# First product of the channel mixing by seven block products in chunks two and three

## The chip, the cores and the metric

The kernel runs on one core of a Trainium2 chip. The metric is the device time of one execution in microseconds (us). The kernel before took 655.24 us, the median of 3 runs (654.52 to 658.01).

Five engines work side by side, each through its own queue in order: PE (matrix products; PEld is its weight load), DVE (vector), ACT (scalar functions, casts, copies), POOL (a second, slower vector engine) and SP (which here only issues DMAs). An engine waits for another by semaphores.

## The reference

Three blocks follow one another on 4 sequences of 576 tokens, 512 channels wide: windowed attention, a gated layer with a spatial product, and a mixer. The change is in the last part of the mixer:

```
def _moe2_ref(x, w_tok1, w_tok2, w_ch1, w_ch2):
    xt = x.transpose(0, 2, 1)
    h = np.maximum(xt @ w_tok1, 0.0) @ w_tok2
    u = x + h.transpose(0, 2, 1)
    h2 = np.maximum(u @ w_ch1, 0.0) @ w_ch2      # w_ch1: 512 x 1536, w_ch2: 1536 x 512
    return (u + h2).astype(np.float32)
```

## The kernel before, in words

Everything is float32. A float32 product is made of three matmuls on rounded words: each operand is split into a high word (ACT rounds it, a CAST) and a low word (DVE subtracts, a TENSOR_TENSOR), and high x high, high x low and low x high are summed in a bank of PSUM (`mm3`, line 155; `split`, lines 141 to 143). The third dimension of a matmul is at most 128, so 512 channels are four steps of three matmuls.

The activations lie in one tile `U`, channels on the partitions, 4 x 2304 tokens. The channel mixing takes the 2304 tokens in three chunks of 768 (`TW`), each in two halves of 384 (`HW`); the chunks are called one, two and three here (c = 0, 1, 2 in the loop of line 760).

In each chunk there are two products. The **first product**, U times W1, is written plainly (`ch1`, lines 722 to 731): W1 has 12 row blocks of 128 (`c1[0..11]`, split once and kept in the tile `ws` for j = 0 to 2 and in tiles `c13`, `c14`, `c15` for j = 3 to 5; block j and block j + 6 lie together), and for each block and each half 12 matmuls of 384 columns go into one of three banks `mm`; ACT takes the bank out with a ReLU (line 729) into a tile `H`. After each j, POOL forms two differences of such tiles (line 734). The **second product**, times W2, already goes by seven block products (`product`, lines 737 to 755): the combinations of W2 were formed beforehand, split, and put in HBM as `scr`; the combinations of the hidden blocks are the differences on POOL. For each of six j a block is split into `oh` (ACT, line 746) and `ol` (DVE, line 747), four buffers each, and six matmuls go into two banks `A` (line 752). The results are added to `U` by DVE or POOL (line 781) and stored.

The weights of the second product come from HBM into the pool `k4`, eight buffers of 128 x 1024 words (line 742). The same pool serves the loading of W1 and W2 before (`load_c1`, `load_c2`, `fetch`), on which DVE works until about 395 us.

The order of instructions up to the end of the attention is written by hand. From there on a scheduler orders each engine's queue when the kernel is built: work that is earlier in the program goes first when its operands and a buffer are there, and later work is put between. In chunks one and two matmuls of the next chunk's first product (line 155) stand between those of the second product (line 752).

Of the kernel before, what the change touches and what calls it, by code (L numbers as in the profile page):

```python
# [20 lines left out]
P = 128  # L21
# [8 lines left out]
def f(ap):  # L30
    return ap.bitcast(F32)
# [3 lines left out]
def tile_kernel(ctx, tc, qT, kT, kE, v, w_in, wsT, b_sp, w_out, w_t1, w_t2, w_c1, w_c2, outT):  # L35
# [20 lines left out]
    bb = const.tile([P, S], F32, name="bb")  # L56
    const.tile([P, 88], F32, name="gap")
# [107 lines left out]
    nat = pool("nat", "right", stack=r_stack, bufs=1)  # L165
    wsp = pool("wsp", "left", bufs=1)
# [475 lines left out]
    scr = tc.dram_tile([8, NJ // 2, P, 2, 2, 256], F32, name="scr")  # L642
    c1 = {}

    def load_c1(j):

        both = ws[:, 2048 * j:2048 * j + 2048] if j < 3 else c1q.tile([P, 2048], F32R, name=f"c1{j}")
        x = k4()
        fetch(x, [w_c1[:, 128 * r:128 * r + 128].rearrange("(k p) c -> p k c", p=P) for r in (j, j + NJ)])
        split(both[:, :1024], both[:, 1024:], x)  # L650
        v = both.rearrange("p (w r k c) -> p w r k c", w=2, r=2, k=4)
        for r in range(2):
            c1[j + NJ * r] = (v[:, 0, r], v[:, 1, r])

# [44 lines left out]
    c1q = pool("c1q", "left", stack=c_stack, bufs=1)  # L699
    up = [pool("up0", "left", stack=c_stack, bufs=1)]  # L700
# [18 lines left out]
    op_ = pool("op", "left", stack=c_stack, bufs=1)  # L719
    Hp = pool("Hp", "right", stack=c_stack, bufs=1)  # L720

    def ch1(u, ft):
# [8 lines left out]
        return out  # L731

# [27 lines left out]
    for c in range(NTOK // TW):  # L760
# [3 lines left out]
        b11, b12, b21, b22, e = [], [], [], [], []  # L764
        for j in range(NJ):
            if c == 0 and j == 0:
                load_c1(5)
                load_c2(5)
            x, y = ch1(u, j)
            b11.append(x)  # L770
            b12.append(y)
            x, y = ch1(u, j + NJ)
            b21.append(x)
            b22.append(y)
            e.append(diff(Hp.tile([P, HW], F32, tag="H", name="H", bufs=30), b12[j], b11[j]))
            diff(b12[j], b22[j], b12[j])
# [121 lines left out]
```

## Time and profile before

| what | value |
| --- | --- |
| median of 3 runs | 655.24 us |
| the profiled execution | 655.88 us, its span 654.0 us |
| mean granted clock of TensorE | 0.990 of full speed |
| busy: PE, DVE, ACT, POOL | 626.1, 407.0, 317.1, 164.0 us |
| first product, chunk one, begins | 366.0 us |
| first product in chunks one to three | 864 matmuls of 128x384 (line 155) |
| second product in chunks one to three | 756 matmuls of 128x384 (lines 752 and 840) |

Busy times are of the whole span. A matmul's own duration in the trace (334 ns) is longer than the distance to the next, since matmuls overlap; what one costs is read from a stretch of them divided by their count. The granted clock is that of PE: 1.00 is the level of 2.4 GHz, 0.50 that of 1.2 GHz.

### The profile page before, as it was taken

What the parts mean: (1) busy time and instruction counts of PE and PEld (TensorE: products, weight loads), DVE (VectorE), ACT (ScalarE), POOL (GpSimd) and SP (SyncE); (2) the same over time, 40 slices, a digit from 0 to 9 for tenths busy, and PEclk for the clock granted to TensorE, in tenths of its full rate; (3) what the DMA queues carried; (4) which work ended last, traced back from release to release, by engine and by line L of the source; (5) the groups of instructions that cost most, each with busy time, mean ns of one, the idle gap of its engine ahead of it and who ended that gap; (6) DMA issues with size and microseconds to landing.
All of it is one profiled execution on the core that took longest, in us unless ns stands there. A gap on an engine that the chain in (4) does not pass through costs nothing.

```text
span 654.0 us, 11885 instructions
## 1 busy us (share of the span) xinstructions
PE 626.1 (96%) x4512; PEld 584.1 (89%) x4512; DVE 407.0 (62%) x861; ACT 317.1 (48%) x809; POOL 164.0 (25%) x172
## 2 busy tenths in 40 slices
PE   6689799999999999999998999999999999999987
PEld 3468699898979898888988999999999999999977
DVE  4786757656485688698899770496300796200892
ACT  4677663535774455566463542454332544232450
POOL 5510000100010010222032164390132570232820
PEclk9889899999999999999998999999999999999999
DMA  8833653322250134534752736177700378500762
GB/s 318 276 96 97 191 165 107 128 74 74 78 174 2 33 115 119 201 113 159 252 184 108 256 114 258 64 217 249 243 0 1 114 215 269 176 1 1 226 215 74
DMA packets 43513, 94.17 MB, mean 144 GB/s; under 512 B 3904, under 2 KB 16448, under 8 KB 43456
## 3 DMA queue, kind: packets, MB, share of 16 engines
q1 hardware_dynamic: 43456, 93.40, 43.1%
q8 instruction: 36, 0.59, 0.4%
q14 instruction: 21, 0.17, 0.1%
HBM read 77.66 MB, written 15.73 MB: 143 GB/s over the span
## 4 chain that ended last, share of the span: by engine, by line
PE 73%; DVE 12%; ACT 7%; DMA 4%; issue 2%; POOL 1%; SPq 0%; DVEq 0%; POOLq 0%; ACTq 0%
PE mm L155 48%; PE A L752 18%; ACT pb L257 3%; DMA k<-in_w_c 3%; PE pt L276 2%; DVE k L68 2%; PE xo L288 1%; DVE k L69 1%; DVE pb L267 1%; DMA U<-in_w_in 1%; POOL k L665 1%; PE sc L234 1%; ACT PT L277 1%; PE A L840 1%; DVE hl L143 1%
## 5 line engine op out<-in xcount | busy, mean ns | idle before, releaser
L747 DVE TENSOR_TENSOR ol<-H,oh 128x384 fp32r<-128x384 f32 x120 | 93.9, 812 | 83.5 <-ACT oh L746 79.0
L734 POOL TENSOR_TENSOR H<-H 128x384 f32<-128x384 f32 x72 | 82.1, 1157 | 147.6 <-ACT H L729 142.2
L752 PE MATMUL A<-oh,w 128*128 128x384 f32 x480 | 108.6, 334 | 0.0
L746 ACT CAST oh<-H 128x384 fp32r<-128x384 f32 x120 | 61.2, 514 | 59.0 <-PE A L752 54.9
L752 PEld LDWEIGHTS A<-oh,w 128*128 128x128 f32 x480 | 85.5, 188 | 0.0
L729 ACT ACTIVATE H<-mm 128x384 f32<-128x384 f32 x72 | 35.1, 491 | 88.6 <-PE mm L155 86.1
L155 PE MATMUL mm<-uh,ws 128*128 128x384 f32 x288 | 76.1, 334 | 0.0
L155 PE MATMUL mm<-uh,c 128*128 128x384 f32 x288 | 73.5, 334 | 0.0
L752 PE MATMUL A<-ol,w 128*128 128x384 f32 x240 | 67.6, 337 | 2.1 <-DVE ol L747 2.1
L155 PE MATMUL mm<-ws,nh 128*128 128x288 f32 x320 | 62.2, 298 | 0.3 <-DVE tmp L385 0.3
L155 PEld LDWEIGHTS mm<-uh,ws 128*128 128x128 f32 x288 | 52.2, 188 | 0.0
L155 PEld LDWEIGHTS mm<-uh,c 128*128 128x128 f32 x288 | 52.0, 188 | 0.0
L155 PEld LDWEIGHTS mm<-ws,nh 128*128 128x128 f32 x320 | 49.9, 188 | 1.1 <-DVE tmp L385 0.6
L354 POOL TENSOR_SCALAR rstd<-mv 128x1 f32<-128x1 f32 x18 | 4.5, 249 | 183.4 <-DVE mv L353 183.2
L155 PE MATMUL mm<-ul,ws 128*128 128x384 f32 x144 | 48.1, 334 | 0.0
L155 PE MATMUL mm<-ul,c 128*128 128x384 f32 x144 | 48.1, 334 | 0.0
L752 PEld LDWEIGHTS A<-ol,w 128*128 128x128 f32 x240 | 43.4, 188 | 3.8 <-DVE ol L747 3.4
L665 POOL TENSOR_TENSOR k<-k 128x256 f32<-128x256 f32 x12 | 13.5, 1136 | 108.3 <-DVE k L69 108.3
L677 DVE TENSOR_TENSOR ul<-U,uh 128x1536 fp32r<-128x1536 f32 x6 | 11.3, 1892 | 43.5 <-PE mm L155 41.7
L155 PE MATMUL mm<-ws,nl 128*128 128x288 f32 x128 | 37.7, 295 | 0.0
L257 ACT ACTIVATE pb<-pb,nm 128x128 f32<-128x128 f32 x96 | 37.2, 398 | 0.4 <-DVE nm L248 0.3
L277 ACT COPY PT<-pt 128x512 f32<-128x512 f32 x36 | 19.5, 591 | 31.2 <-PE pt L276 31.2
(131 smaller groups left out, 1424.7 us busy)
## 6 DMA issues: line engine op xcount, KB each, us to landing
w<-scr SPq DMA_DIRECT2D x63, 512.0 KB, 4.2
k<-in_w_c SPq DMA_DIRECT2D x24, 512.0 KB, 6.4
scr<-hl SPq DMA_DIRECT2D x18, 512.0 KB, 4.1
kk<-in_kT SPq DMA_DIRECT2D x16, 384.0 KB, 4.8
qq<-in_qT SPq DMA_DIRECT2D x18, 256.0 KB, 4.2
va<-in_v SPq DMA_DIRECT2D x18, 256.0 KB, 2.8
vb<-in_v SPq DMA_DIRECT2D x18, 256.0 KB, 3.7
outT<-U SPq DMA_DIRECT2D x24, 192.0 KB, 3.6
```

The lines of the kernel that those rows point to most:

```text
L68: nc.vector.scalar_tensor_tensor(out=y, in0=high, scalar=-0x80000000, in1=y, op0=ALU.bitwise_and, op1=ALU.bitwise_or)
L155: nc.tensor.matmul(o, a, c, start=(i == 0), stop=(i == n - 1))
L257: nc.scalar.activation(out=pb[:, h, :], in_=scs[g][:, h - 4 * g, :] if mk is None else pb[:, h, :], func=AF.Exp, scale=SCALE if mk is None ...
L276: nc.tensor.transpose(pt[:, h, :], pb[:, 4 * g + h, :], ident)
L277: nc.scalar.copy(out=PT[:, 4 * g:4 * g + 4, :], in_=pt)
L665: nc.gpsimd.tensor_tensor(out=blk(o), in0=blk(a), in1=blk(b), op=op)
L677: nc.vector.tensor_tensor(out=ul, in0=us, in1=f(uh), op=ALU.subtract)
L729: nc.scalar.activation(out=t, in_=ps, func=AF.Relu)
L734: nc.gpsimd.tensor_tensor(out=out, in0=a, in1=b, op=ALU.subtract)
L746: nc.scalar.copy(out=oh, in_=blk[j])
L747: nc.vector.tensor_tensor(out=ol, in0=blk[j], in1=f(oh), op=ALU.subtract)
L752: nc.tensor.matmul(acc[d], a, m, start=(first and j == 0 and i == 0), stop=(last and j == NJ - 1 and i == 2), skip_group_check=True)
```

## The change

In chunks two and three the first product too is made by seven block products instead of eight. With W1 seen as 2 x 2 blocks (channels and rows halved: a11, a12, a21, a22 for row blocks j and j + 6) and the chunk's U as 2 x 2 blocks (x11, x21, x12, x22: channels and token halves), four combinations of W1 and four of U are needed. Each block product is two steps of three matmuls (`seven`). Chunk one stays as it was, since the combinations of W1 are made while it runs.

What is added: `sum_c1`, in chunk one, puts W1's blocks together again from their words and forms the four combinations s1 to s4 on DVE, six times, and stores them as float32 in HBM (`sums`). `load_sums` fetches them in chunks two and three and splits them. `usums` forms t1 to t4 of U on DVE and splits them; their words go where they find room: in the half of the second input tile that is no longer split plainly, in the places of a21 in `ws` and `c1b`, and in a small new pool. `ch1_seven` runs the products: banks a and c are from `mm`, b is from `A`; a first product in each bank is read out (ACT copies it as p1, DVE adds p1 and keeps x and z) before a second is summed on top. To make room, `bb` moves to another pool, the tiles of W1 for j = 3 to 5 become one tile, and a gap shrinks. The lines of the changed kernel are shifted: `seven` is 782, the additions of DVE 807 to 826, the second product 848 and 853.

```diff
-        both = ws[:, 2048 * j:2048 * j + 2048] if j < 3 else c1q.tile([P, 2048], F32R, name=f"c1{j}")
+        both = c1_words(j)
...
+    def sum_c1(j):
+        hl = f(c1_words(j))
+        x, y = [k4() for _ in range(2)]
+        nc.vector.tensor_tensor(out=x, in0=hl[:, :1024], in1=hl[:, 1024:], op=ALU.add)
+        a11, a12, a21, a22 = [x[:, 256 * i:256 * i + 256] for i in range(4)]
+        s1, s2, s3, s4 = [y[:, 256 * i:256 * i + 256] for i in range(4)]
+        for o, a, b, op in ((s1, a21, a22, ALU.add), (s3, a11, a21, ALU.subtract), (s2, s1, a11, ALU.subtract), (s4, a12, s2, ALU.subtract)):
+            nc.vector.tensor_tensor(out=o, in0=a, in1=b, op=op)
+        nc.sync.dma_start(out=sums[j], in_=y.rearrange("p (s c) -> p s c", s=4))
+
+    def load_sums(j):
+        x = k4()
+        nc.sync.dma_start(out=x.rearrange("p (s c) -> p s c", s=4), in_=sums[j])
+        h, l = [kp.tile([P, 1024], F32R, tag="k4", name=n, bufs=8) for n in ("sh", "sl")]
+        split(h, l, x)
...
-        nc.scalar.copy(out=uh, in_=us)
-        nc.vector.tensor_tensor(out=ul, in0=us, in1=f(uh), op=ALU.subtract)
+        k0 = 2 if c and h else 0
+        split(uh[:, k0:], ul[:, k0:], us[:, k0:])
         return uh, ul
+
+    def usums(c, u):
...
+        t1, t2, t3, t4 = [k4()[:, :2 * HW].rearrange("p (k c) -> p k c", k=2) for _ in range(4)]
+        for i, o, a, b in ((0, t1, x12, x11), (1, t2, x22, t1), (2, t3, x22, x12), (3, t4, x21, t2)):
+            nc.vector.tensor_tensor(out=o, in0=a, in1=b, op=ALU.subtract)
+            split(*homes[i], thirds(o))
...
+    def seven(o, ws2, us2, first):
+        todo = [x for (sh, sl), (mh, ml) in zip(ws2, us2) for x in ((sh, mh), (sh, ml), (sl, mh))]
+        for i, (a, m) in enumerate(todo):
+            nc.tensor.matmul(o, a, m, start=first and i == 0, stop=i == len(todo) - 1, skip_group_check=True)
...
+    def ch1_seven(X):
+        x11, x21, x22, t1, t2, t3, t4 = X
+        S = [load_sums(j) for j in range(2)]
+        outs, left = [], []
+        for j in range(NJ):
+            if j and j + 1 < NJ:
+                S.append(load_sums(j + 1))
+            s1, s2, s3, s4 = S[j]
+            a, c = [psmm.tile([P, 512], F32, tag="mm", name="mm")[:, :HW] for _ in range(2)]
+            b = psA.tile([P, 512], F32, tag="A", name="A")[:, :HW]
...
+            seven(a, a11, x11, True)
+            p1 = op_.tile([P, HW], F32, tag="p1", name="p1", bufs=2)
+            nc.scalar.copy(out=p1, in_=a)
+            seven(b, s2, t2, True)
+            for step in left:
+                step()
+            x, z = [op_.tile([P, HW], F32, tag=t, name=n, bufs=4) for t, n in (("oh", "x"), ("ol", "z"))]
+            nc.vector.tensor_tensor(out=x, in0=b, in1=p1, op=ALU.add)
+            seven(c, s1, t1, True)
+            nc.vector.tensor_tensor(out=z, in0=c, in1=p1, op=ALU.add)
+            seven(a, a12, x21, False)
+            nc.scalar.activation(out=h11, in_=a, func=AF.Relu)
+            seven(b, s3, t3, False)
+            def total(o, bank, more):
+                nc.vector.tensor_tensor(out=o, in0=bank, in1=more, op=ALU.add)
+                nc.scalar.activation(out=o, in_=o, func=AF.Relu)
+            total(h22, b, z)
+            seven(c, s4, x22, False)
+            total(h12, c, x)
+            e = diff(H(), h12, h11)
+            diff(h12, h22, h12)
+            def last(b=b, a22=a22, h21=h21, p1=p1):
+                seven(b, a22, t4, False)
+                nc.vector.tensor_tensor(out=h21, in0=b, in1=p1, op=ALU.add)
+                nc.scalar.activation(out=h21, in_=h21, func=AF.Relu)
+            left = [last]
...
+        if c:
+            b11, b12, b21, b22, e = ch1_seven(usums(c, u))
+        else:
...
+                if j:
+                    sum_c1(j - 1)
+            sum_c1(NJ - 1)
```

Up to the middle of chunk one the queue of every engine keeps its order. From there on they differ, at three places as follows.

DVE's queue of the kernel before, at the end of chunk one's first product (`hl` are W2's words for HBM, `ol` low words for the second product, `ul` those of chunk two's input):

```order
L143 TENSOR_TENSOR hl<-k_4528,hl 128x256
L143 TENSOR_TENSOR hl<-k_4528,hl 128x2x256
L747 TENSOR_TENSOR ol<-H,oh 128x384
L143 TENSOR_TENSOR hl<-k_4529,hl 128x2x256 x2
L747 TENSOR_TENSOR ol<-H,oh 128x384
L677 TENSOR_TENSOR ul<-U,uh 128x1536 x2
L747 TENSOR_TENSOR ol<-H,oh 128x384 x11
```

The same place in the changed kernel, where the combinations of W1 (lines 663 and 667, the last of six shown) have been put in:

```order
L667 TENSOR_TENSOR k_4903<-k_4903,k_4902 128x256
L667 TENSOR_TENSOR k_4974<-k_4973 128x256 x2
L663 TENSOR_TENSOR k_4981<-c1b 128x1024
L667 TENSOR_TENSOR k_4903<-k_4902,k_4903 128x256
L667 TENSOR_TENSOR k_4974<-k_4974,k_4973 128x256
L667 TENSOR_TENSOR k_4982<-k_4981 128x256 x2
L667 TENSOR_TENSOR k_4974<-k_4973,k_4974 128x256
L667 TENSOR_TENSOR k_4982<-k_4982,k_4981 128x256
L667 TENSOR_TENSOR k_4982<-k_4981,k_4982 128x256
L142 TENSOR_TENSOR ul<-U,uh 128x1536
L142 TENSOR_TENSOR ul<-U,uh 128x768
L848 TENSOR_TENSOR ol<-H,oh 128x384 x11
```

Six groups of five additions now stand ahead of the two splits of the next input and of the fifth low word of the second product; the second of these splits is half as wide.

DVE's queue of the kernel before, in the sixth block product of chunk one (low words, here with their numbers, and additions to `U`):

```order
L747 TENSOR_TENSOR ol_5312<-H_4604,oh_5311 128x384
L747 TENSOR_TENSOR ol_5322<-H_4667,oh_5321 128x384
L747 TENSOR_TENSOR ol_5334<-H_4730,oh_5333 128x384
L781 TENSOR_TENSOR U_84<-A_5237,U_84 128x384
L781 TENSOR_TENSOR U_84<-A_5238,U_84 128x384
L747 TENSOR_TENSOR ol_5344<-H_4793,oh_5343 128x384
L747 TENSOR_TENSOR ol_5356<-H_4856,oh_5355 128x384
L747 TENSOR_TENSOR ol_5366<-H_4919,oh_5365 128x384
L747 TENSOR_TENSOR ol_5382<-H_4619,oh_5381 128x384
```

The same place in the changed kernel (line 720 forms T; `ul_5504` is the low word of t1):

```order
L848 TENSOR_TENSOR ol_5362<-H_4606,oh_5361 128x384
L720 TENSOR_TENSOR k4_5509<-U_83 128x768
L848 TENSOR_TENSOR ol_5372<-H_4669,oh_5371 128x384
L848 TENSOR_TENSOR ol_5384<-H_4740,oh_5383 128x384
L888 TENSOR_TENSOR U_83<-A_5287,U_83 128x384
L142 TENSOR_TENSOR ul_5504<-k4_5509,uh_5503 128x768
L888 TENSOR_TENSOR U_83<-A_5288,U_83 128x384
L720 TENSOR_TENSOR k4_5510<-U_83,k4_5509 128x768
L848 TENSOR_TENSOR ol_5394<-H_4811,oh_5393 128x384
L848 TENSOR_TENSOR ol_5406<-H_4882,oh_5405 128x384
L720 TENSOR_TENSOR k4_5511<-U_83 128x768
L848 TENSOR_TENSOR ol_5416<-H_4953,oh_5415 128x384
```

T's eight instructions stand between the low words of the last two block products, one by one; the first four are seen here.

PE's queue of the kernel before, in the last block product of chunk one (`mm` is the next chunk's first product):

```order
L752 MATMUL A_5237<-oh_5403,w_5401 128x384 x2
L752 MATMUL A_5238<-oh_5403,w_5401 128x384 x2
L752 MATMUL A_5237<-ol_5404,w_5401 128x384
L752 MATMUL A_5238<-ol_5404,w_5401 128x384
L752 MATMUL A_5237<-oh_5413,w_5401 128x384 x2
L752 MATMUL A_5238<-oh_5413,w_5401 128x384 x2
L155 MATMUL mm_5502<-ul_5454,ws_98 128x384
L155 MATMUL mm_5502<-uh_5453,ws_98 128x384
L752 MATMUL A_5237<-ol_5414,w_5401 128x384
L752 MATMUL A_5238<-ol_5414,w_5401 128x384
L752 MATMUL A_5237<-oh_5425,w_5423 128x384 x2
L752 MATMUL A_5237<-ol_5426,w_5423 128x384
```

The changed kernel, from the third row block of that product on:

```order
L853 MATMUL A_5287<-oh_5453,w_5451 128x384 x2
L853 MATMUL A_5288<-oh_5453,w_5451 128x384 x2
L782 MATMUL A_5539<-ws_98,sh_5527 128x384 x2
L782 MATMUL mm_5538<-uh_5503,sh_5527 128x384
L782 MATMUL mm_5538<-ul_5504,sh_5527 128x384
L782 MATMUL mm_5600<-uh_5499,ws_98 128x384
L782 MATMUL mm_5600<-ul_5500,ws_98 128x384
L782 MATMUL mm_5600<-uh_5499,ws_98 128x384 x2
L782 MATMUL mm_5600<-ul_5500,ws_98 128x384
L782 MATMUL mm_5600<-uh_5499,ws_98 128x384
L853 MATMUL A_5287<-ol_5454,w_5451 128x384
L853 MATMUL A_5288<-ol_5454,w_5451 128x384
```

The matmuls put between are now ten at once, four on the first sums (`sh`) and six on the first input block of the second row block.

## Rows read from the trace of the kernel before

**Rows 1.** Page, busy time of each engine (share of the span) and instructions:
```profile
PE 626.1 (96%) x4512; PEld 584.1 (89%) x4512; DVE 407.0 (62%) x861; ACT 317.1 (48%) x809; POOL 164.0 (25%) x172
```

**Rows 2.** Windows: start:end, length, busy (count) per engine, clock, DMA:
```profile
408.00:414.00 6.00, 6.00 (x36) 6.00 (x35) 0.00 (x0) 1.27 (x3) 2.03 (x2) 1.00 0.00 0
...
426.00:432.00 6.00, 6.00 (x36) 6.00 (x35) 6.00 (x6) 2.59 (x6) 6.00 (x6) 1.00 0.77 238
...
450.00:456.00 6.00, 6.00 (x36) 6.00 (x36) 3.63 (x7) 3.20 (x7) 0.00 (x0) 1.00 0.69 207
...
480.00:486.00 6.00, 6.00 (x36) 6.00 (x35) 0.25 (x1) 1.48 (x3) 1.52 (x2) 1.00 0.00 0
...
618.00:624.00 6.00, 5.27 (x29) 4.51 (x27) 6.00 (x5) 2.27 (x5) 6.00 (x6) 1.00 0.69 236
...
624.00:630.00 6.00, 4.62 (x23) 3.99 (x24) 6.00 (x12) 4.44 (x10) 1.31 (x2) 1.00 0.41 153
```

**Rows 3.** Chain that ended last: start us, us, engine, tile, line, instructions:
```profile
354.80 61.28 PE mm L155 x360
...
561.90 41.60 PE mm L155 x240
...
620.50 1.37 DVE ol L143
```

**Rows 4.** Waits of PE, 355 to 654 us: total us, times, longest:
```profile
PE A L752 <- DVE ol L747: 2.1, 4, 0.7
```

**Rows 5.** Tiles ol and U: count: duration ns min/median/max, first and last start:
```profile
L747 DVE TENSOR_TENSOR ol<-H,oh x120: 541/559/1416, 370.0 to 640.4; 128x384 fp32r<-128x384 f32 x120
L781 DVE TENSOR_TENSOR U<-A,U x36: 540/548/558, 433.1 to 650.5; 128x384 f32<-128x384 f32 x36
```

**Rows 6.** Groups by form: count, busy us, mean ns, idle before and releaser:
```profile
L143 DVE TENSOR_TENSOR ws<-k,ws 128x1024 fp32r<-128x1024 f32 x3 | 3.7, 1217 | 0.0
...
L143 DVE TENSOR_TENSOR c<-k,c 128x1024 fp32r<-128x1024 f32 x3 | 4.5, 1491 | 0.3 <-ACT c L142 0.3
...
L143 DVE TENSOR_TENSOR t_l<-k,t_h 128x512 fp32r<-128x512 f32 x2 | 1.4, 682 | 0.0
...
L143 DVE TENSOR_TENSOR t_l<-k,t_h 128x256 fp32r<-128x256 f32 x1 | 0.4, 419 | 0.0
...
L143 DVE TENSOR_TENSOR hl<-k,hl 128x256 fp32r<-128x256 f32 x6 | 4.2, 707 | 0.0
...
L142 ACT CAST ws<-k 128x1024 fp32r<-128x1024 f32 x3 | 3.2, 1054 | 3.5 <-DVE k L69 3.5
...
L729 ACT ACTIVATE H<-mm 128x384 f32<-128x384 f32 x72 | 35.1, 491 | 88.6 <-PE mm L155 86.1 <-POOL H L734 2.4
...
L791 ACT COPY p<-A 128x384 f32<-128x384 f32 x6 | 2.8, 477 | 1.0 <-PE A L752 1.0
```

**Rows 7.** Timeline of DVE: start us, us, instruction, count, idle before it:
```profile
390.93 2.11 DVE L143 TENSOR_TENSOR hl<-k,hl 128x512 fp32r<-128x512 f32 x2 [3.91 <-ACT hl L142]
...
394.30 1.00 DVE L747 TENSOR_TENSOR ol<-H,oh 128x384 fp32r<-128x384 f32 x1 [1.26 <-ACT oh L746]
...
415.92 1.76 DVE L677 TENSOR_TENSOR ul<-U,uh 128x1536 fp32r<-128x1536 f32 x1 [20.62 <-PE mm L155]
...
425.37 7.84 DVE L747 TENSOR_TENSOR ol<-H,oh 128x384 fp32r<-128x384 f32 x6 [0.48 <-PE A L752]
```

**Rows 8.** Window of line L155 (first product) alone, 420 to 444 us:
```profile
420.00:444.00 24.00, 6.97 (x30) 5.26 (x30) 1.00 0.63 200
```

**Rows 9.** Windows around the idle time of PE before 356 us:
```profile
352.00:354.00 2.00, 0.83 (x7) 0.78 (x6) 2.00 (x5) 0.15 (x1) 0.10 (x1) 1.00 0.00 0
354.00:356.00 2.00, 1.49 (x8) 1.25 (x7) 2.00 (x6) 0.88 (x2) 1.92 (x3) 0.70 0.00 0
356.00:358.00 2.00, 2.00 (x10) 2.00 (x10) 1.43 (x2) 0.94 (x2) 1.57 (x2) 0.50 0.34 132
```

**Rows 10.** DMA issues: tensors, queue, count, KB each, median us to landing:
```profile
w<-scr SPq DMA_DIRECT2D x63, 512.0 KB, 4.2
```

More of the change, by code (lines that the diff above doesn't have):

```diff
@@ L55, in tile_kernel @@
     nc.gpsimd.memset(mhalf, -0.5)
-    bb = const.tile([P, S], F32, name="bb")
-    const.tile([P, 88], F32, name="gap")
+    const.tile([P, 24], F32, name="gap")
     U = const.tile([P, 4, NTOK], F32, name="U")
@@ L642, in tile_kernel, with c1_words @@
     scr = tc.dram_tile([8, NJ // 2, P, 2, 2, 256], F32, name="scr")
+    sums = tc.dram_tile([NJ, P, 4, 256], F32, name="sums")
     c1 = {}
+    def c1_words(j):
+        return (ws if j < 3 else c1b)[:, 2048 * (j % 3):2048 * (j % 3) + 2048]
     def load_c1(j):
-        both = ws[:, 2048 * j:2048 * j + 2048] if j < 3 else c1q.tile([P, 2048], F32R, name=f"c1{j}")
+        both = c1_words(j)
         x = k4()
@@ L653, in load_c1 @@
             c1[j + NJ * r] = (v[:, 0, r], v[:, 1, r])
+    def sum_c1(j):
[12 more added lines that the diff above has]
+        split(h, l, x)
+        return [[(h[:, 256 * i + 128 * k:256 * i + 128 * k + 128], l[:, 256 * i + 128 * k:256 * i + 128 * k + 128]) for k in range(2)] for i in range(4)]
     def load_c2(j):
@@ L719, in tile_kernel @@
     op_ = pool("op", "left", stack=c_stack, bufs=1)
+    tq = pool("tq", "left", stack=c_stack, bufs=1)
     Hp = pool("Hp", "right", stack=c_stack, bufs=1)
@@ L731, in ch1, with H @@
         return out
+    def seven(o, ws2, us2, first):
+        todo = [x for (sh, sl), (mh, ml) in zip(ws2, us2) for x in ((sh, mh), (sh, ml), (sl, mh))]
+        for i, (a, m) in enumerate(todo):
+            nc.tensor.matmul(o, a, m, start=first and i == 0, stop=i == len(todo) - 1, skip_group_check=True)
+    def H():
+        return Hp.tile([P, HW], F32, tag="H", name="H", bufs=30)
+    def ch1_seven(X):
[8 more added lines that the diff above has]
+            b = psA.tile([P, 512], F32, tag="A", name="A")[:, :HW]
+            a11, a12, a22 = [[(c1[r][0][:, k, :], c1[r][1][:, k, :]) for k in ks] for r, ks in ((j, (0, 1)), (j, (2, 3)), (j + NJ, (2, 3)))]
+            h11, h12, h21, h22 = [H() for _ in range(4)]
+            seven(a, a11, x11, True)
[24 more added lines that the diff above has]
+            left = [last]
+            outs.append((h11, h12, h21, h22, e))
+        left[0]()
+        return [list(x) for x in zip(*outs)]
@@ L763, in tile_kernel @@
         u += [uin(c, h) for h in range(len(u), 2)]
[L764 to L776, printed above, removed]
+        if c:
+            b11, b12, b21, b22, e = ch1_seven(usums(c, u))
+        else:
+            b11, b12, b21, b22, e = [], [], [], [], []
+            for j in range(NJ):
+                if j == 0:
+                    load_c1(5)
+                    load_c2(5)
+                x, y = ch1(u, j)
+                b11.append(x)
+                b12.append(y)
+                x, y = ch1(u, j + NJ)
+                b21.append(x)
+                b22.append(y)
+                e.append(diff(H(), b12[j], b11[j]))
+                diff(b12[j], b22[j], b12[j])
+                if j:
+                    sum_c1(j - 1)
+            sum_c1(NJ - 1)
         us = [[U[:, 2 * dh:2 * dh + 2, t0 + HW * h:t0 + HW * h + HW] for h in range(2)] for dh in range(2)]
```

13 lines of the change are left out of this document (added).

## The prediction

> **What bounds the kernel now.** I read the page first, then the span cut into windows, then the chain that ended last, then the waits of TensorE. The page gives PE 96% of the span [rows 1]. In the windows the reader is to see that from about 366 us on PE is busy for the whole of nearly every stretch at a granted clock of 1.00, while DVE goes from nothing (408 to 414) to all of its time (426 to 432) and back to almost nothing (480 to 486) [rows 2]. The chain says the same: it is PE alone from 354.80 us on, broken only in the last chunk, and 240 matmuls of the first channel product take 41.60 us, so one costs 0.1733 us whenever nothing delays it [rows 3]. The waits of PE after 355 us hold one entry of weight: 2.1 us in 4 waits of the second product for DVE's low words, all four in the last chunk, the only one without the matmuls of a next chunk to put in between [rows 2, 4]. So this part of the kernel is a queue of matmuls: 540 for a chunk (288 in the first product, 252 in the second), and a matmul less is worth 0.1733 us as long as the other engines keep PE fed.
>
> **The change part by part.** Dropping multiplications: the first product of a chunk before is 12 row blocks times 2 halves times 12 matmuls, 288. Now it is 6 times 7 block products of 6 matmuls, 252, of the same 384 columns. Over two chunks that is 72 matmuls less: 72 x 0.1733 = 12.48 us [rows 3]. No matmul is added anywhere, and chunk one keeps its 288. This is the whole of the gain, and everything below is what may be paid back.
>
> The combinations of W1 (chunk one): DVE gets six times a 1024-wide addition and four 256-wide ones. With 1.217 us for 1024 columns and 0.419 for 256 that is 6 x (1.217 + 4 x 0.419) = 17.4 us; with the dearest rows of these widths (1.491 and 0.707) it is 25.9 us [rows 6]. In the order they stand ahead of the splits of chunk two's input and of the fifth low word of the second product. DVE stood idle there from the end of its split at 395.3 us to 415.92 us, 20.6 us, and could begin some 2 us earlier [rows 7]. At the lower price they are over by about 411 us and cost nothing; at the upper one they end some 3 to 5 us after 416. Behind the last of them wait the input's splits, then the fifth low word. PE has four blocks of the second product ready, 4 x 6 x 0.1733 = 4.2 us, and the 6 matmuls of chunk two that need only the first input block; the second input split is half as wide as before, which gives back 0.9 us. So about 2 us of delay is covered, and what can show is 0 to 4 us. I take 0.5, near the lower price, because POOL is mostly idle there: from 408 to 414 it has 2.03 of 6 us [rows 2]. The six stores of the sums go to SP's queue ahead of the weights of the second product; those land 4.2 us after issue [rows 10] and have 20 us.
>
> Less to put in between: while POOL works without a pause, a low-word split takes 1.3 us (six in 7.84 us from 425.37) in place of its median 0.559 [rows 5, 7], which is more than the 1.04 us PE needs for the block. Before, PE filled the time with matmuls of the next chunk, 30 between 420 and 444 us [rows 8]. Now there are 12, since the other six products need operands that are formed later. The nearest row for a chunk without any such filling is the last chunk, which lost 2.1 us [rows 4], with two of the final block's extra splits in the same stretch. Bounds per chunk are 0 and 2.1 us; below nothing is excluded, since PE is full there already. With 12 matmuls (2.1 us) left, and without the extra splits, I am near nothing: 0.5 for each of chunks one and two, 1.0 in all.
>
> Forming T (at the end of chunks one and two): per chunk DVE gets four subtractions and four splits 768 wide, less half of one input split, and the first two splits of W1's sums. A 768-wide one lies between 0.682 (512) and 1.217 (1024) [rows 6], 0.95 in the middle: 8 x 0.95 + 2 x 1.217 = 10.0 us, next to 12 low-word splits (6.7 us) and four additions to the residual (2.2 us) during the last two products of the chunk. That is 18.9 us of DVE against 12.5 us of second-product matmuls and 28 matmuls of chunk two that the order puts there, 4.9 us: 17.4. POOL has nothing in that stretch (0.00 from 450 to 456) [rows 2], and PE enters it with up to four blocks in hand, which is 4.2 us. So the deficit of 1.5 us is covered on paper; an early subtraction in front of a low word can still show. Bounds per chunk 0 and 3.7 us (if 768 columns cost as much as 1024 beside a busy POOL, 8 x (1.491 - 0.95) = 4.3 more, and only half the lead is there, 2.1); I take 0.75, so 1.5 in all.
>
> The seven products themselves (chunks two and three): a bank now goes PE, DVE, PE up to three times. Per row block DVE gets five additions with one operand in PSUM and a 1024-wide split: 5 x 0.55 + 1.217 = 4.0 us, and ScalarE a copy, four ReLUs and a 1024-wide cast: 0.477 + 4 x 0.491 + 1.054 = 3.5 us [rows 5, 6], against 42 x 0.1733 = 7.3 us of PE. Both fit. The additions out of PSUM are the right kind: that form takes 540 to 558 ns in all 36 runs, POOL busy or not, while the split of two SBUF operands goes from 541 to 1416 [rows 5]. The order leaves 12 or more matmuls, 2.1 us, between a product into a bank and the next one into it, where the addition and its place in DVE's queue (a 1.2 us split ahead of it at worst) take 1.8 us. Bounds: nothing, and the longest single wait of the last chunk, 0.7 us [rows 4], in each of 12 row blocks, 8.4. I take 0.75 a chunk, 1.5 in all, nearer to the row of the additions.
>
> The loads of the sums, six a chunk, stand in SP's queue behind the stores of finished outputs and ahead of the next chunk's weights, whose prefetch was done during the first product with all eight buffers free. Now the buffers come free as sums are used up. The first weights are wanted some 40 us after the stage begins and the last sums are split well before, so 4.2 us of landing [rows 10] are hidden; if not, one landing a chunk, 8.4 us, shows.
>
> Sum: 12.48 - 0.5 - 1.0 - 1.5 - 1.5 = 8.0 us. The profiled execution took 655.88 us (span 654.0), so it would take 647.9; the median of the runs shown is 0.64 lower, 655.24, and the forecast 647.2.
>
> **The rivals.** First, everything is covered: PE stays full in chunks two and three, and 12.5 us are kept, with at most 2.5 lost: 642.8 to 645.2. For it speaks that PE lost nothing in chunks one and two before, with DVE at 6.00 of 6 us; against it that the margins above are a few matmuls wide, where they were dozens.
>
> Second, the gain is eaten: each of the 12 row blocks shows one wait of 0.7 us, and the T's and the landing of weights add their upper bounds in part: 8.4 + 3 to 5 us paid, 655.24 - 12.5 + 11.4 to 13.4 = 654.1 to 656.1. For it speaks the strict order on DVE, where an addition PE needs stands behind casts it does not need yet; against it the half-empty DVE (4.0 of 7.3 us).
>
> Third, the other side: the clock. Where PE idled 1.68 us between 352 and 356 us, its granted clock read 0.70 and then 0.50 in the 4 us from 354 on [rows 9], the lower level of 1.2 GHz: 0.6 + 1.0 = 1.6 us more, so that such a gap costs 3.3 us. If the round trips of the seven products open one gap of that size in every second row block, six in all, 20 us are paid: 655.24 - 12.5 + 20 = 662.7, slower; it decides from five such gaps on. Against it: the four waits of the last chunk, 0.7 us at the longest, left the clock at 1.00 [rows 2, 4], and the order has other products at hand. The Trainium skill (TensorE: Matmul & The Clock Gate, "A second HAM failure mode: psum-queue depth-cycling") holds that cycling through PSUM banks with small idles between groups of matmuls makes the clock swing between its levels; taken at its word it speaks for this rival even with gaps of 0.7 us, and the last chunk's trace, with the clock at 1.00, does not agree for four of them.
>
> That the change does not do what it says can be left out for the multiplications: the order of the changed program has 252 matmuls there.
>
> **How the numbers follow.** What a measurement of this kernel can tell from no change is about 0.5%, 3.3 us: faster means under 651.9, slower over 658.5. The forecast (645.2 to 651.9) has 0.55, the first rival 0.22, the second with its neighbourhood (651.9 to 658.5) 0.14, the third 0.09. So faster 0.77, same 0.14, slower 0.09. The range runs from 643.3, where of all costs only some 0.5 us shows, to 653.0, a little into the second rival; some 0.04 lie below it and 0.16 above.
>
> **What would show it.** Right: 252 matmuls of the first product in some 44 us in chunks two and three, where 288 took 50; PE waits for DVE of 2 to 6 us beside the old 2.1; the clock at 1.00; DVE busy from 393 to about 412 us without PE noticing; the 128x384 additions out of PSUM at 0.55 us. Wrong: PE waits on the new additions of 0.5 us and more in each row block, a granted clock under 1.00 after 420 us, low-word splits of the last two products late behind the T's by more than 2 us, or PE waiting for weights or sums to land.

## The result and the profile after

The changed kernel takes **648.73 us**, the median of 4 runs (648.16 to 650.56), against 655.25 us for the kernel before (654.52 to 658.01): a ratio of 0.9898, 95% interval 0.9863 to 0.9933. The profiled execution took 650.56 us, its span 648.4 us, at a mean granted clock of 0.989.

**The whole.** The page of the changed kernel, busy time of each engine, share of the span and instructions:

```profile
PE 617.8 (95%) x4440; PEld 571.0 (88%) x4440; DVE 489.7 (76%) x979; ACT 337.2 (52%) x841; POOL 171.1 (26%) x172
```

TensorE has 72 matmuls less than in [rows 1], and DVE 82.7 us more work. What this bought is best measured over one stretch, from the end of chunk one's first product to the end of the span, since ahead of it PE does the same work in both programs. The chain that ended last, of the changed kernel (start, duration, engine, tile, line, instructions):

```profile
356.87 61.28 PE mm L154 x360
```

Chunk one's first product ends at 356.87 + 61.28 = 418.15 us; before it ended at 354.80 + 61.28 = 416.08 us [rows 3]. The stretch behind it was 654.0 - 416.1 = 237.9 us and is 648.4 - 418.15 = 230.25 us: **7.7 us shorter** (forecast 8.0). The piece of 360 matmuls that the first product ends takes the same 61.28 us; it begins 2.1 us later, for a reason that lies ahead of it. Windows around that start, of the changed kernel (start:end, length, busy and count of PE, PEld, DVE, ACT and POOL, granted clock, DMA share, GB/s):

```profile
352.00:354.00 2.00, 0.67 (x6) 0.44 (x4) 2.00 (x4) 0.32 (x1) 0.00 (x0) 1.00 0.00 0
354.00:356.00 2.00, 0.70 (x5) 0.70 (x6) 2.00 (x5) 0.08 (x1) 0.02 (x1) 1.00 0.00 0
356.00:358.00 2.00, 1.49 (x9) 1.26 (x8) 2.00 (x6) 0.95 (x2) 1.92 (x3) 0.85 0.00 0
358.00:360.00 2.00, 2.00 (x11) 2.00 (x10) 1.78 (x4) 0.85 (x2) 1.66 (x2) 0.50 0.34 131
```

PE is idle for 3.14 of the 6 us up to 358, and then the clock is granted at 0.85 and 0.50; in [rows 9] the same gap held 1.68 us. The queues of both programs are the same there, and the chain names the late data: a load of W1 that was issued 0.35 us later and took 1.73 us longer to land, which makes the 2.1 us. Its piece of the chain, before and after:

```profile
337.53 5.26 DMA k<-in_w_c
337.88 6.99 DMA k<-in_w_c
```

So this is one execution's late data and not the change. A second profiled execution of the changed kernel (first run below) ended the same product at 411.59 us, and its stretch behind it was 641.7 - 411.59 = 230.1 us. It had a gap too: PE was busy for 0.55 and 1.49 us of the two windows of 2 us from 348, so 1.96 us idle, but there the granted clock stayed at 1.00. The end of that product moves by 6.6 us between two executions of one program; the stretch agrees to 0.2.

**The stretch, in order.** Windows of the changed kernel, columns as above:

```profile
414.00:420.00 6.00, 6.00 (x36) 6.00 (x36) 4.84 (x9) 3.98 (x6) 3.17 (x2) 1.00 0.92 267
420.00:426.00 6.00, 6.00 (x37) 6.00 (x36) 5.44 (x6) 2.89 (x7) 3.19 (x3) 1.00 1.02 417
...
438.00:444.00 6.00, 5.92 (x32) 5.14 (x31) 6.00 (x8) 2.85 (x6) 3.37 (x3) 1.00 0.68 238
...
450.00:456.00 6.00, 6.00 (x37) 6.00 (x35) 5.86 (x10) 4.05 (x8) 0.00 (x0) 1.00 0.33 126
456.00:462.00 6.00, 6.00 (x36) 6.00 (x36) 6.00 (x11) 5.09 (x9) 0.00 (x0) 1.00 0.36 115
...
480.00:486.00 6.00, 6.00 (x36) 5.88 (x36) 3.59 (x8) 3.58 (x7) 2.03 (x2) 1.00 0.00 0
...
516.00:522.00 6.00, 6.00 (x29) 4.57 (x28) 6.00 (x6) 3.18 (x7) 6.00 (x5) 1.00 0.76 246
522.00:528.00 6.00, 5.30 (x30) 4.64 (x29) 6.00 (x7) 2.11 (x5) 6.00 (x6) 1.00 0.52 173
...
612.00:618.00 6.00, 5.08 (x25) 3.94 (x25) 6.00 (x7) 0.93 (x2) 6.00 (x5) 1.00 0.62 210
618.00:624.00 6.00, 4.45 (x24) 3.81 (x23) 6.00 (x12) 5.12 (x12) 1.35 (x2) 1.00 0.37 122
```

The reader is to look at the counts behind PE, not at its busy time: a full window of 6 us holds 36 or 37 matmuls. From 516 to 522 us PE is "busy" for all of it and still issues 29. Where W1's combinations (414 to 420), T (450 to 462) and the seven products (480 to 486) were feared, the windows are full; where the second product's low words are made beside a working POOL, they are not. Summed over neighbouring windows, chunk one lacks 5 matmuls (0.9 us), chunk two some 17 (3.0 us) and chunk three some 26 (4.6 us). Before, only chunk three lacked any: 29 and 23 in the two windows of [rows 2] against 36.5 full, 21 in all or 3.6 us. The granted clock is 1.00 in all of these. DVE is busy for the whole of the windows with the fewest matmuls (438, 516, 522, 612, 618), so it does not stand there waiting for differences that POOL delivers late.

The waits of PE in the changed kernel, 355 to 654 us (total us, times, longest):

```profile
PE A L853 <- DVE ol L848: 3.2, 5, 1.2
PE mm L154 <- DVE U L639: 3.1, 2, 2.6
```

The first line answers to [rows 4]: the same wait, 1.1 us longer. It shows 3.2 us where the counts show 8.5 lost. The second line is the gap before the first product. What was lost stands in another list, the waits of the weight load (PEld); from 410 us to the end, of the changed kernel and of the kernel before:

```profile
PEld A L853 <- DVE ol L848: 8.9, 20, 1.5
PEld A L752 <- DVE ol L747: 3.4, 4, 1.0
```

It is PE's weight load that waits for the low words, 8.9 us in 20 waits where the counts say 8.5, and 3.4 before where they say 3.6.

The groups by form in the changed kernel (count, busy us, mean ns, idle before and releaser):

```profile
L848 DVE TENSOR_TENSOR ol<-H,oh 128x384 fp32r<-128x384 f32 x120 | 98.9, 863 | 7.4 <-ACT oh L847 6.6 <-ACT p L898 0.6
L835 POOL TENSOR_TENSOR H<-H 128x384 f32<-128x384 f32 x72 | 89.3, 1257 | 136.2 <-ACT H L816 103.1 <-ACT H L775 28.2 <-DVE ol L848 4.0
...
L888 DVE TENSOR_TENSOR U<-A,U 128x384 f32<-128x384 f32 x36 | 18.6, 550 | 8.3 <-PE A L947 4.1 <-PE A L853 3.9
...
L720 DVE TENSOR_TENSOR k<-U 128x768 f32<-128x768 f32 x4 | 3.8, 953 | 0.5 <-PE A L853 0.5
```

Low words (median 558 ns, as in [rows 5]) have a mean of 863: a part of them takes twice as long or more (1407 ns at most). Additions to `U` with an operand in PSUM stay at 550, and T's subtractions at 953, as estimated. POOL's stretch and what DVE does beside it, in chunk two (start, us, instruction, count, idle before), first POOL:

```profile
501.24 7.40 POOL L835 TENSOR_TENSOR H<-H 128x384 f32<-128x384 f32 x5 [3.98 <-ACT H L816]
509.13 6.83 POOL L835 TENSOR_TENSOR H<-H 128x384 f32<-128x384 f32 x5 [0.49 <-DVE ol L848]
515.93 7.75 POOL L888 TENSOR_TENSOR U<-p,U 128x384 f32<-128x384 f32 x6
523.64 7.46 POOL L835 TENSOR_TENSOR H<-H 128x384 f32<-128x384 f32 x6
```

then DVE:

```profile
512.89 11.21 DVE L848 TENSOR_TENSOR ol<-H,oh 128x384 fp32r<-128x384 f32 x9
524.02 1.01 DVE L888 TENSOR_TENSOR U<-A,U 128x384 f32<-128x384 f32 x2
524.95 7.03 DVE L848 TENSOR_TENSOR ol<-H,oh 128x384 fp32r<-128x384 f32 x6
```

POOL runs 30 us with a single pause of 0.49. Nine low words take 11.21 us, 1.25 each, and six of POOL's additions 7.75, 1.29 each: beside each other, each engine finishes one every 1.25 to 1.3 us. PE needs 1.04 us for the six matmuls of one low word, so DVE can't keep up, and the additions to `U` between them, 0.55 us, are not touched. In the kernel before, most of POOL's differences of this chunk came one or two at a time while the plain first product ran, and the unbroken stretch behind them was 16 us:

```profile
510.45 1.81 POOL L734 TENSOR_TENSOR H<-H 128x384 f32<-128x384 f32 x1 [3.21 <-ACT H L729]
514.43 2.55 POOL L734 TENSOR_TENSOR H<-H 128x384 f32<-128x384 f32 x2 [2.16 <-DVE ol L747]
519.04 7.46 POOL L781 TENSOR_TENSOR U<-p,U 128x384 f32<-128x384 f32 x6 [2.06 <-ACT p L791]
526.47 8.74 POOL L734 TENSOR_TENSOR H<-H 128x384 f32<-128x384 f32 x7
```

Of the chunk's 24 differences 16 lie in the unbroken stretch of the changed kernel, from 501.24 on, and 10 lay behind 510.45 before: POOL carries more of them on into the second product. That the seven products finish the hidden blocks later is read from the program; it was not tried.

### The profile page after: what moved, and what is told of

Its sections match the earlier page's. It is cut to its first block, busy times and chain, and to the rows that moved or that the text cites. A ratio compares the mean times of both kernels' runs of the same rounds, so it can differ in the third digit from the quotient of the medians.

```text
span 648.4 us, 11947 instructions
## 1 busy us (share of the span) xinstructions
PE 617.8 (95%) x4440; PEld 571.0 (88%) x4440; DVE 489.7 (76%) x979; ACT 337.2 (52%) x841; POOL 171.1 (26%) x172
## 4 chain that ended last, share of the span: by engine, by line
PE 62%; DVE 17%; DMA 7%; ACT 7%; issue 4%; POOL 1%; SPq 1%; DVEq 0%; POOLq 0%; ACTq 0%
PE mm L154 27%; PE A L853 16%; PE mm L782 8%; PE A L782 6%; DMA k<-in_w_c 4%; ACT pb L257 4%; DVE ol L848 2%; DVE k L67 2%; DVE k L68 2%; PE pt L276 2%; PE xo L288 2%; DVE gl L598 1%; DVE pb L267 1%; POOL k L688 1%; DMA raw<-in_wsT 1%
## 5 line engine op out<-in xcount | busy, mean ns | idle before, releaser
L835 POOL TENSOR_TENSOR H<-H 128x384 f32<-128x384 f32 x72 | 89.3, 1257 | 136.2 <-ACT H L816 103.1
L848 DVE TENSOR_TENSOR ol<-H,oh 128x384 fp32r<-128x384 f32 x120 | 98.9, 863 | 7.4 <-ACT oh L847 6.6
L265 DVE TENSOR_SCALAR rs<-sm 128x8 f32<-128x8 f32 (+1 forms) x19 | 3.7, 196 | 47.5 <-ACT pb L257 47.5
L71 ACT ACTIVATE k<-k 128x512 f32<-128x512 f32 (+2 forms) x31 | 19.7, 645 | 28.5 <-DMA k<-in_w_c 22.9
L154 PE MATMUL mm<-xh,wi_h 128*128 128x384 f32 x96 | 32.7, 341 | 0.7 <-ACT vf L348 0.6
L154 PE MATMUL mm<-xh,wi_l 128*128 128x384 f32 x96 | 32.1, 335 | 0.0
L154 PE MATMUL mm<-xl,wi_h 128*128 128x384 f32 x96 | 32.1, 334 | 0.0
L154 PE MATMUL mm<-gh,wo_h 128*128 128x512 f32 (+1 forms) x80 | 29.7, 375 | 0.0
L154 PE MATMUL mm<-gl,wo_h 128*128 128x512 f32 (+1 forms) x80 | 29.6, 370 | 0.0
L154 PE MATMUL mm<-gh,wo_l 128*128 128x512 f32 (+1 forms) x80 | 29.5, 369 | 0.0
```

The lines of the kernel that those rows point to most:

```text
L71: nc.scalar.activation(out=x, in_=f(high), func=AF.Copy, scale=DOWN)
L154: nc.tensor.matmul(o, a, c, start=(i == 0), stop=(i == n - 1))
L835: nc.gpsimd.tensor_tensor(out=out, in0=a, in1=b, op=ALU.subtract)
L848: nc.vector.tensor_tensor(out=ol, in0=blk[j], in1=f(oh), op=ALU.subtract)
```

## The experiments

Theory: the 72 matmuls are saved in full, and what is paid back comes from one place, DVE's low words beside POOL. Rivals: the new places of the tiles, the round trips of the banks, or T have a price of their own. Stretches are measured as above, from the end of chunk one's first product in each run's profile.

**The changed kernel again**, unaltered, beside the next experiments.

> The changed kernel once more, unaltered, as the base on this chip for the runs beside it. Theory and rivals alike: 648 to 649 us if this chip is like the first, 0.988 to 0.992 of the kernel before.

650.22 us (643.83 to 652.48, 10 runs), ratio 0.9916 [0.9882, 0.995] to the kernel before on that chip (654.74); the time is 1.2 us above the expected 649, the ratio inside the expected range. The profiled execution, 643.83, is the shortest of the ten and the one told of above: with a stretch of 230.1 us, what it is ahead by lies before the stretch. Differences of 2 us between medians of different chips are not read below; stretches are.

**The places alone.** The first product is plain in all chunks; tiles, pools and lines are those of the changed kernel.

```diff
-        k0 = 2 if c and h else 0
+        k0 = 0
...
-        if c:
+        if False:
             b11, b12, b21, b22, e = ch1_seven(usums(c, u))
...
-                if j:
-                    sum_c1(j - 1)
-            sum_c1(NJ - 1)
```

> The changed kernel with the plain first product in all three chunks, so that of the change only the new places of tiles are left (the bias row in another pool, the smaller gap, W1's last three blocks in one tile). Theory (the new places cost nothing, and the 2 us by which the profiled execution after began the first product later is one late load of W1): as the kernel before, 655.2 us, at most 1 us off, and the first product beginning within 1 us of 366.0. Rival (the new places delay the stage before the mixing): 657.3 us, every run some 2 us above the kernel before.

654.62 us (650.78 to 656.93, 10 runs), ratio 1.0 [0.9973, 1.0026]. Stretch 653.3 - 415.28 = 238.0 us, before 237.9. The new places cost nothing, the rival's 657.3 is out, and the later start of the first product does not come from them.

**The six additions of POOL left out** in each chunk (the first block product's share of the output is then missing in three of its quarters).

```diff
-        for d in range(2):
-            p1 = op_.tile([P, HW], F32, tag="p1", name="p1", bufs=2)
-            nc.scalar.copy(out=p1, in_=A[d])
-            for dh, h in ((0, 1), (1, 1), (1, 0)):
-                accum(dh, h, d, p1, nc.gpsimd)
```

> The changed kernel without the six additions to U on POOL in each chunk (left out: the first block product is not added to three of the four quarters of the output), with their two copies on ScalarE. Theory (what is lost of the 12.5 us is lost where POOL and DVE work on SBUF together in the second product, 0.9, 3.0 and 4.6 us in chunks one to three): 7.5 us of POOL a chunk are gone, the low words there go back to 0.55 us, PE's waits fall under 2 us in all, and the time is 642 to 644 us. Rival (the loss comes from the new work on DVE, the T's and the round trips of the seven products): these are untouched, 647.5 to 649 us.

639.44 us (638.59 to 646.78, 5 runs), ratio 0.9783 [0.9758, 0.9807]: a larger gain than the theory's 642 to 644, and the rival's 647.5 to 649 is out. In chunk two every window is full again; in chunk three one still lacks 7 matmuls. The profiled execution, 646.78, is the longest of the five, and shows a price that neither profile of the changed kernel has. Its wait of PE and two windows:

```profile
PE A L853 <- DMA w<-scr: 2.7, 1, 2.7
```

```profile
414.00:420.00 6.00, 5.14 (x30) 4.82 (x28) 5.85 (x8) 4.00 (x6) 2.52 (x2) 1.00 0.84 249
420.00:426.00 6.00, 4.15 (x17) 4.15 (x18) 2.40 (x5) 1.02 (x2) 2.21 (x2) 0.77 1.02 416
```

The stores of W1's sums and the weights of the second product go out together, and the DMA engines are full; the weights came late, PE stood for 2.7 us, and the clock was granted at 0.77 in the window with the wait's end: some 26 matmuls fewer than two full windows hold, 4.5 us. The execution is 6 to 8 us longer than the other four, which were not profiled, so the rest of that is open. Its stretch is 644.9 - 417.05 = 227.9 us with these 4.5 in it.

**The same six additions by DVE, straight from PSUM.**

```diff
-            p1 = op_.tile([P, HW], F32, tag="p1", name="p1", bufs=2)
-            nc.scalar.copy(out=p1, in_=A[d])
             for dh, h in ((0, 1), (1, 1), (1, 0)):
-                accum(dh, h, d, p1, nc.gpsimd)
+                accum(dh, h, d, A[d])
```

> The changed kernel with those six additions on DVE, straight from the PSUM bank, so that nothing is left out. Theory (contention with POOL): DVE gets 6 x 0.55 = 3.3 us more a chunk but six low words get 0.75 us shorter, 4.5 us, and POOL is free 7.5 us earlier for the differences: 644.5 to 647 us. Rival (DVE's amount of work in that stretch is what counts, with or without POOL): 3.3 us more in each chunk where DVE is full, 651 to 655 us.

645.61 us (645.06 to 646.55, 4 runs), ratio 0.9878 [0.9859, 0.9897]: inside the theory's 644.5 to 647, and the rival's 651 to 655 is out. Stretch 643.5 - 416.4 = 227.1 us, 3.1 less than the changed kernel's. Chunk one is full but for a wait of 0.2 us for weights at its start; one window of chunk two (28 matmuls) and three of chunk three (32, 29, 29) are not. DVE has six additions, 3.3 us, more to do in each chunk, and PE still loses less.

**x and z added twice**: six times two more additions out of PSUM in each of chunks two and three, 6.6 us of DVE, inside the round trip of the banks.

```diff
-            nc.vector.tensor_tensor(out=x, in0=b, in1=p1, op=ALU.add)
+            for _ in range(2):
+                nc.vector.tensor_tensor(out=x, in0=b, in1=p1, op=ALU.add)
             seven(c, s1, t1, True)
-            nc.vector.tensor_tensor(out=z, in0=c, in1=p1, op=ALU.add)
+            for _ in range(2):
+                nc.vector.tensor_tensor(out=z, in0=c, in1=p1, op=ALU.add)
```

> The changed kernel with the two additions that stand between two products into one bank (x and z) each done twice, 1.1 us of DVE more in each of the 12 row blocks, on the way from PE to DVE and back to PE. Theory (the seven products have slack, DVE is busy some 26 of 42 us there): no change beyond 1 us, 647.5 to 649.5. Rival (the round trips are tight and part of what is lost): 0.55 to 1.1 us a row block, 655 to 662 us.

650.64 us (649.62 to 654.65, 10 runs), ratio 0.9951 [0.9927, 0.9974]: 2.3 to 3.5 us more than the changed kernel's two ratios give, with intervals that overlap. The profiled stretch is clearer: 647.8 - 412.2 = 235.6 us, 5.4 more than the changed kernel's. The theory's "no change beyond 1 us" fell, and the rival's 655 to 662 did not come either. Its waits of PE from 415 us on:

```profile
PE A L855 <- DVE ol L850: 3.6, 7, 0.8
PE A L782 <- ACT sh L141: 2.5, 2, 1.5
PE A L855 <- DMA w<-scr: 1.9, 1, 1.9
```

None of them is on x or z (lines 807 to 811), and the windows inside the seven products are full (36 or 37 matmuls): the round trips held with twice the additions. What shows is the first sums (`sh`) at the hand-over from the second product to the seven, once in each of chunks two and three, where the counts lack some 18 matmuls, 3.1 us; and once the late weights again, some 12 matmuls or 2.2 us. The doubling did not test the hand-over alone, so why the first sums are late in this order is not shown.

**T formed twice**: the four subtractions of line 720, 0.95 us each, are repeated, 3.8 us of DVE in each of two chunks.

```diff
-            nc.vector.tensor_tensor(out=o, in0=a, in1=b, op=ALU.subtract)
+            for _ in range(2):
+                nc.vector.tensor_tensor(out=o, in0=a, in1=b, op=ALU.subtract)
             split(*homes[i], thirds(o))
```

> The changed kernel with each of the four subtractions that form the T's done twice: 4 x 0.95 = 3.8 us of DVE more at the end of chunks one and two, where POOL is idle and PE stayed full. Theory (forming the T's is covered, some 3.7 us of DVE are idle between 444 and 474 us): 0 to 1.5 us a chunk, 648 to 651 us. Rival (the T's stand on the path already and their doubling shows in full): 3.8 us a chunk, 656 us.

655.25 us (652.48 to 657.48, 10 runs), ratio 1.0012 [0.9986, 1.0037], 5.0 us above the changed kernel on that chip: my expectation of 648 to 651 fell. The time is near the rival's 656, but the doubling does not show in full, as the rival has it: stretch 651.3 - 415.2 = 236.1 us, 5.8 more, of 2 x 3.8 = 7.6 put in. Windows of this kernel where T is formed in chunk one:

```profile
450.00:456.00 6.00, 5.88 (x34) 5.57 (x33) 6.00 (x11) 2.97 (x7) 0.00 (x0) 1.00 0.18 66
456.00:462.00 6.00, 5.01 (x29) 4.69 (x28) 6.00 (x11) 3.25 (x6) 0.00 (x0) 1.00 0.45 153
462.00:468.00 6.00, 5.72 (x34) 5.23 (x32) 4.63 (x7) 2.16 (x3) 0.00 (x0) 1.00 0.53 145
```

The changed kernel had 37, 36 and 37 there. T costs nothing as it is, and by this estimate has about (7.6 - 5.8) / 2 = 0.9 us to spare in a chunk.

**Half of POOL's differences on DVE too** (on top of the additions: lines with b11, b22 and b21, b11).

```diff
         for j in range(NJ):
-            diff(b11[j], b22[j], e[j])
+            ddiff(b11[j], b22[j], e[j])
...
-            diff(b21[j], b21[j], b11[j])
+            ddiff(b21[j], b21[j], b11[j])
```

> The kernel with the POOL additions on DVE, and besides the twelve differences of b11 and b21 in each chunk on DVE. Theory (a POOL instruction costs DVE about 0.75 us by holding up a split, a difference on DVE itself costs 0.55): another 2.4 us a chunk of DVE gained, PE's waits under 2 us, 642 to 645 us. Rival (DVE's own amount decides, 6.6 us more a chunk in the full stretch): 649 to 656 us.

643.67 us (642.64 to 644.27, 4 runs), ratio 0.9834 [0.9794, 0.9874]: inside the theory's 642 to 645, and the rival's 649 to 656 is out. Stretch 642.0 - 417.55 = 224.45 us. Low words have a mean of 589 ns.

**All of them on DVE, POOL without work in the mixing.**

```diff
     def diff(out, a, b):
-        nc.gpsimd.tensor_tensor(out=out, in0=a, in1=b, op=ALU.subtract)
+        nc.vector.tensor_tensor(out=out, in0=a, in1=b, op=ALU.subtract)
...
-                accum(dh, h, d, p1, nc.gpsimd)
+                accum(dh, h, d, A[d])
```

> The same with all 24 differences of a chunk on DVE, POOL without work in the mixing. Theory (no contention left, every low word at 0.55 us; DVE in the seven products rises from some 26 to 33 of 42 us): 642 to 645 us, within 1.5 us of the run with twelve. Rival (round trips of the seven products get behind the differences in DVE's queue): 648 us or more.

640.38 us (638.08 to 642.35, 4 runs), ratio 0.9785 [0.9737, 0.9832]: below the theory's 642 to 645, and the rival's 648 is out. Once more on another chip:

> The changed kernel with POOL's work of the channel mixing on DVE once more, to stand beside the two others of this job on one chip. It should repeat 640.4 within 1.5 us. Theory: against the plain first product with the same edit the seven products then show nearly all of the 72 matmuls, 11 to 12.5 us. Rival (the two edits gain the same time twice over): 4 to 7 us only.

639.17 us (636.74 to 642.87, 6 runs), ratio 0.976 [0.973, 0.979]: **9 to 10 us below the changed kernel, and in the two runs 14.4 and 16.5 below the kernel before on the same chip.** The groups of the second of these profiles:

```profile
L848 DVE TENSOR_TENSOR ol<-H,oh 128x384 fp32r<-128x384 f32 x120 | 63.7, 557 | 7.5 <-ACT oh L847 5.4 <-PE A L853 1.9
L835 DVE TENSOR_TENSOR H<-H 128x384 f32<-128x384 f32 x72 | 38.9, 552 | 1.8 <-ACT H L816 1.5
L888 DVE TENSOR_TENSOR U<-A,U 128x384 f32<-128x384 f32 x54 | 27.3, 551 | 10.3 <-PE A L853 6.8 <-PE A L945 3.4
```

and its windows at two of the places where the changed kernel had 29 and 25 matmuls:

```profile
516.00:522.00 6.00, 6.00 (x36) 6.00 (x35) 5.86 (x13) 3.83 (x8) 0.00 (x0) 1.00 0.77 259
612.00:618.00 6.00, 6.00 (x36) 6.00 (x36) 5.63 (x13) 2.99 (x6) 0.00 (x0) 1.00 0.90 311
```

DVE took over 72 differences (38.9 us) and 18 additions (8.7 us more of the third group), and lost 35.2 us of low words, 98.9 to 63.7, and 6.3 of W1's combinations. The durations of all its instructions add up to 529.9 us, against 530.4 and 527.1 in the two executions of the changed kernel: in sum the work taken over cost DVE next to nothing. PE and its weight load wait for nothing after the first product begins, and each window is full. Stretch 636.6 - 414.72 = 221.9 us, 8.3 less than the changed kernel's; what the medians differ by beyond that is inside their spread. It is 1260 matmuls x 0.1733 = 218.4 and 3.5 us behind the last one.

**The kernel before with the same edit**: plain first product, POOL's work on DVE.

> The kernel before, with its plain first product, but with POOL's 72 differences and 18 additions of the channel mixing done by DVE (the additions straight out of PSUM). Theory (POOL stretches DVE's low-word splits, and this costs TensorE time only where no matmuls of a plain product are left to put in between): before lost only about 3.6 us, all in chunk three, so the time falls by 2 to 3.6 us, to 651 to 653, and the low words take 0.55 us throughout. Rival (POOL beside DVE costs the same whichever way the first product is made): the 9 to 10 us that the same edit gave the changed kernel appear here too, 645 to 646.5.

652.2 us (649.0 to 653.12, 7 runs), ratio 0.9942 [0.992, 0.9964]. The theory's 651 to 653 holds; the rival's 645 to 646.5 is out. Its low words, and the piece of the chain that ends with the first product:

```profile
L747 DVE TENSOR_TENSOR ol<-H,oh 128x384 fp32r<-128x384 f32 x120 | 65.0, 559 | 43.3 <-ACT oh L746 27.4 <-PE A L752 15.0
```

```profile
356.55 57.36 PE mm L155 x342
```

Stretch 648.3 - 413.91 = 234.4 us, 3.5 less than before: the 21 matmuls missing in its last chunk, and no more. In chunks one and two POOL stretched the low words as well [rows 7], and the matmuls put between covered it: the windows there were full. On the same chip the seven products then take 652.2 to 639.17, 13.0 us, and the stretch 234.4 to 221.9, **12.5 us: 72 x 0.1733, whole.**

**T formed twice without POOL.** The edit of T above, on the kernel without POOL's work.

> The changed kernel with POOL's work of the channel mixing on DVE, and with the four subtractions that form T done twice in chunks two and three (3.8 us more of DVE in each). Theory (forming T has about 1.5 us to spare, whatever POOL does, since POOL is idle in that stretch; what goes over shows on TensorE): 3 to 6 us above the same kernel with T formed once, 643 to 647, with TensorE waiting for DVE or for the first sums at the hand-over. Rival (the room was small only because DVE came late out of the stretch beside POOL): at most 1.5 us above, 639 to 642.

643.78 us (642.91 to 646.5, 5 runs), 4.6 above the same kernel with T formed once, inside the theory's 3 to 6, and the rival's 639 to 642 is out; stretch 641.9 - 414.33 = 227.6, 5.7 more. The room of T is the same 0.9 to 1.0 us with or without POOL.

## Why the prediction was right, and which terms were not

The time was forecast at 647.2 us within 643.3 to 653.0 and measured at 648.73; the sum of 8.0 us stands against 7.7 in the stretch of the trace. But it was put together from terms that were wrong on both sides and met: 4.5 us of cost forecast over four places, and 4.9 measured in one of them. The mechanism of the gain was right; that the sum came so close was luck.

- **The dropped multiplications, 12.48 us:** right; 12.5 between the two kernels without POOL's work.
- **The combinations of W1, 0.5:** 0 on PE in the changed kernel. They took 4.5 + 3.6 us for the six wide additions and 14.6 for the 24 narrow ones, 22.7 in all, nearer to the upper price of 25.9 than to 17.4, and ended at 416.87 us. The split of the next input behind them then stood 1.13 us more for PE's first product, so they held up nothing. The step that called the stores and the weights behind them hidden was too light: DMA share rises to 0.92 and 1.02 from 414 to 426 us (0.14 and 0.39 before), and in two experiments the weights were late, by 1.9 and 2.7 us.
- **Less to put in between, 1.0 in all:** this is the term that was mis-sized. It measured 0.9 in chunk one, 3.0 in chunk two and 1.0 more than before in chunk three, 4.9 us. Two things made it small in the forecast. Its bound of 2.1 us a chunk came from the waits [rows 4], while the counts of [rows 2], which stood beside it, give 3.6 us for the same place: the waits of the weight load, 3.4 us there, are not in PE's waits. And it took POOL's stretch as it was before; the seven products hand POOL its differences late, and in chunk two the unbroken stretch grew from 16 to 30 us. How the 3.0 us divide between this and the fewer matmuls in between was not tried; both need POOL beside DVE, without which nothing is lost.
- **Forming T, 1.5:** 0, with 0.9 us to spare in a chunk. The 0.95 us for 768 columns were right, and no upper bound came true since POOL is idle there; the deficit on paper, 1.5 us against 4.2 of lead, left 2.7, three times the room that there was.
- **The round trips, 1.5:** 0. The additions out of PSUM took 0.55 us, and twice as many of them still made PE wait for none.
- **The loads of the sums:** 3.3 us to land, in time in the changed kernel; with more work on DVE at the hand-over (x and z twice, T twice) PE waited for the first of them.
- **The rivals:** "everything covered" is what the kernel without POOL's work does, at 639 to 640, below that rival's 642.8 to 645.2 since the old loss of 3.5 us goes as well. "The gain is eaten" did not come: none of PE's waits in the changed kernel is on the round trips. For the third rival, the clock stayed at 1.00 from the end of the first product to the last matmul, with five waits of up to 1.2 us. The Trainium skill (TensorE: Matmul & The Clock Gate, "A second HAM failure mode: psum-queue depth-cycling") would have it swing when banks are cycled with small idles between; this trace does not agree. That rival's price of 3.3 us for a gap of 1.68 us is not a fixed one either: after 1.96 us of idle in 4 us the second execution's clock stayed at 1.00. What decides that was not tried.

That POOL is what stretches the low words is shown by the runs. How it does so is not shown; a rule of the Trainium skill fits (SBUF — State Buffer, "Who interferes with whom"): a DVE instruction with two inputs in SBUF contends with a POOL instruction that reads SBUF, for a read port that only one of them has at a time, and a DVE instruction with a single input in SBUF does not. The trace agrees in which instructions are stretched, and in the order: in the changed kernel POOL starts at 513.34, 514.64 and 515.93 us and DVE between, at 513.72, 515.02 and 516.31, while the additions with one operand in PSUM keep their 0.55 us. It does not give the size: alone, low words follow one another every 0.47 us (five in 2.42 us from 532.84) and POOL's differences every 0.98 (two in 1.99 us from 477.17, kernel before), 1.45 together, which is more than the 1.29 measured, so neither engine is shut out for the whole of the other's instruction.

## What to carry to other kernels

Count the matmuls in windows where an engine feeds PE closely, and read the waits of the weight load beside PE's own: a PE that is "busy" 6.00 of 6 us at 29 matmuls is losing time, and PE's waits showed 3.2 us of 8.5. Before work is taken from an engine that is always full, ask what that work was covering elsewhere: here the plain product's matmuls, put between, covered that POOL doubled the time of DVE's splits, and shrinking the product laid it open. A second engine that reads SBUF beside a DVE that reads two operands there was no free help here: take its work away once and time it.

## What the runs showed of the hardware

A subtraction of two 128x384 float32 operands in SBUF took 0.55 us on DVE alone and 1.25 us in a run of nine beside a POOL that did the like, with POOL at 1.29 there; an addition with one operand in PSUM kept its 0.55 us. Giving POOL's 72 differences and 18 additions, 112.6 us of its time, to DVE cost DVE 47.6 us in its groups and gave 41.5 back in low words and W1's combinations alone. That an engine's work can be moved onto the busier one and leave that one's total on the page no higher (489.7 and 486.7 us in two executions of the changed kernel, 483.0 and 482.2 in the two runs without POOL) I had not expected.
